# A fifth token tile routed by VectorE rows, and 18 places for expert weight pieces, in an attention, MLP and mixture-of-experts kernel

## The chip, the cores and the metric

One core of one Trainium2 chip. The metric is the device time of one execution in microseconds, of which the median over several runs is quoted. All arithmetic that matters is done at about fp32 accuracy: a large operand is split into a high part and a low part (names ending in `h` and `l`, or slices 0 and 1), and a product is three matmuls, high by high, high by low and low by high.

Engines: TensorE (PE: matmuls and transposes), VectorE (DVE), ScalarE (ACT), GpSimd (POOL) and SyncE (SP, which here issues the weight DMAs). Each of them runs its own instructions in the order in which they were built, and waits at an instruction whose inputs or buffers are not ready.

## The reference

Causal attention for 2 batches of 12 heads, 448 positions of 64; its output is x, 896 tokens of 768. Then a dense MLP, then a layer of eight experts, top one:

```python
h = np.maximum(x @ w_in, 0.0)              # 896 x 2048
x = h * h @ w_out                          # 896 x 768
xn = x / (np.linalg.norm(x, axis=-1, keepdims=True) + 1e-06)
en = expert_emb / (np.linalg.norm(expert_emb, axis=-1, keepdims=True) + 1e-06)
logits = xn @ en.T / tau                   # 896 x 8
expert_idx = np.argmax(logits, axis=1)
# gate_w: the softmax probability of the chosen expert
for e in range(E):
    mask = expert_idx == e
    h = np.maximum(x[mask] @ w1[e], 0.0)   # 768 -> 1024
    out[mask] = gate_w[mask, None] * (h @ w2[e])
```

## The kernel before

**Stages.** Attention and the first MLP matmul fill the first half of the time. The second MLP matmul (`b_tiles`) goes over seven tiles of 128 tokens: tiles 0 and 1 together, then tiles t = 2 to 6 one pass each. A pass has 16 steps f; a step is three pairs of matmuls, each 128x384 (`yps`, L639). After a pass ACT copies the sums to `ysb` (L648). After the passes come the experts, slot by slot (`hps`, `ops`).

**Routing.** A tile is routed by a generator, `route_tile` and then `choose`, whose PE instructions are put between the steps of the passes: tile t-1's logits are made in pass t, and its ranks follow in that pass or the next. A tile listed in `CFG["dve"]` gets its eight logits on DVE: eight instructions, each the product of the tile with one embedding row that is spread over all partitions (`rows`, L662). Any other tile gets them on PE: six transposes (`yt`, L672), a split of `yt` into `yhl` (ACT cast, DVE low part), six matmuls (`lgt`, L696), a DVE copy (`lgs`, L699) and two transposes (`lg`, L703). `choose` then takes the tile's norm by Newton steps (`norm_of`, L575 to L590, ten short DVE instructions after the start values), scales (`sc`, L712 to L715), finds the maximum `m`, lets ACT take the exponentials (`ex`, L720), and makes the one-hot rows `OH` (L725). PE counts ranks from `OH` (`rk`, L728), DVE reads them (`c8`, L740, and `ranks`).

**The early expert.** After the first five tiles (NE = 5) the expert with the most tokens among them is taken (`early`): PE counts (`cnt`, L794), DVE finds the expert's number `eidx` (L805) and which of its tokens go where (`oc`, L817; `rv`, L760), PE makes a table (`tabp`, L773), POOL gathers the tokens, and SP loads the expert's weights, whose number it reads from `eidx`. All that lies in passes 5 and 6, so that this expert's first matmuls (`hps`, slot "D") can follow the last pass at once.

**Weight pieces.** An expert's weights come in 16 pieces, two per DMA of 768 KB (`pieces`). ACT rounds a piece to its high part (`mh`), DVE makes the low part (`ml`). Each piece has a place, the buffers that a `w_out` piece held before, so there are 16. `pace` and `freed` limit how many pieces of later experts are fed ahead of the matmuls that read them.

**What sets the order.** PE's order is written out by hand: `CFG["rs"][t]` lists pairs (f, u), "at step f of pass t take the next part of tile u's routing"; `et` does that for `early` (steps of pass 5), `xe` for the gathered tokens and `ew` for weight pieces (steps of pass 6). The order on DVE, ACT, POOL and SP in these passes is made when the kernel is built, by a scheduler with its own model of durations; `urgent` raises the priority of routing, and `issue_after(last["oh"])` keeps the logits of a tile behind the `OH` of the tile before. The chunks `hs` are the MLP's hidden values of one tile and a quarter of the 16 steps, split by ACT and DVE (`h2_split`, L65 and L72) into one of four rotating buffers: the split for the next use of a buffer waits for the step that last reads it.

Of the kernel before, what the change touches and what calls it, by code (L numbers as in the profile page):

```python
# [8 lines left out]
F32 = mybir.dt.float32  # L9
# [23 lines left out]
def f32(ap):  # L33
# [20 lines left out]
def build(tc, qkd, vd, w_in, w_out, emb, tau, wm, cst, out, dbg_y=None):  # L54
# [452 lines left out]
    def wo_load():  # L507
        f = len(wo)
        wo.append(w_load(w_out, f, slots[woslot[f]], f"wo{f}", "woh", "wol"))

    def h2_split(t, q):

        hs = hpool.tile([P, 2, 4, P], F32R, tag="hs", bufs=4, name="hs")
        p0 = t * P
        at = p0
        while at < p0 + P:
            g = at // GT
            end = min(p0 + P, (g + 1) * GT)
# [103 lines left out]
    def b_tiles(ts, hooks={}):  # L622
        ps = {t: [ps_y.tile([P, 512], F32, tag=f"y{c}", name="yps") for c in range(2)] for t in ts}
        for f in range(NF):
            for x in hooks.get(f, ()):
                next(x, None)
            for _ in range(CFG["ew"].count(f) if -1 in hooks else 0):

                with ExitStack() as es:
                    if f > CFG["rt6"][3]:  # L630
                        es.enter_context(tc.issue_after(last["oh"].ins))
                    for _ in range(2):
                        next(hooks[-1], None)
# [156 lines left out]
    def early():  # L790
# [61 lines left out]
    def pieces(s, res):  # L852

        for i2 in range(8):
# [39 lines left out]
    def pace(x, cap=2.7):  # L894
# [241 lines left out]
    for t in range(2, NTI):  # L1136
# [10 lines left out]
        if t == NTI - 1:  # L1147
# [302 lines left out]
```

## Time and profile before

| | us |
|---|---|
| median of 3 runs (542.78 to 543.02) | 542.87 |
| the profiled execution | 543.2 |
| its span | 541.5 |
| PE busy | 527.2 (97%) |
| DVE busy | 413.5 (76%) |
| ACT busy | 287.4 (53%) |
| POOL busy | 205.6 (38%) |

The span is what the profile's times count from and to; the profiled execution is 1.7 us longer than its span and 0.3 us longer than the median. Starts below are microseconds from the start of the span. Pass 3 begins at 274.4, pass 4 at 291.5, pass 5 at 308.3, pass 6 at 328.2, and the early expert's matmuls at 348.3; PE's last matmul is at 532.8.

### The profile page before, as it was taken

What the parts mean: (1) busy time and instruction counts of PE and PEld (TensorE: products, weight loads), DVE (VectorE), ACT (ScalarE), POOL (GpSimd) and SP (SyncE); (2) the same over time, 40 slices, a digit from 0 to 9 for tenths busy, and PEclk for the clock granted to TensorE, in tenths of its full rate; (3) what the DMA queues carried; (4) which work ended last, traced back from release to release, by engine and by line L of the source; (5) the groups of instructions that cost most, each with busy time, mean ns of one, the idle gap of its engine ahead of it and who ended that gap; (6) DMA issues with size and microseconds to landing.
All of it is one profiled execution on the core that took longest, in us unless ns stands there. A gap on an engine that the chain in (4) does not pass through costs nothing.

```text
span 541.5 us, 9616 instructions
## 1 busy us (share of the span) xinstructions
PE 527.2 (97%) x3374; PEld 496.2 (92%) x3374; DVE 413.5 (76%) x976; ACT 287.4 (53%) x635; POOL 205.6 (38%) x273
## 2 busy tenths in 40 slices
PE   7899999999999999999999999999999999999993
PEld 4799999889999999999999989999999999999992
DVE  7888899656887979597899776895296897983741
ACT  7889887315335242433332326631386887764651
POOL 7998899916635643231011201026201302400010
PEclk9999999999999999999999999999999999999998
DMA  5667674331546555358200019303978889984310
GB/s 183 177 156 170 146 230 111 117 117 58 176 131 217 167 183 176 120 174 274 79 30 30 16 31 408 159 2 110 346 231 274 266 281 364 272 279 154 119 53 7
DMA packets 28474, 89.22 MB, mean 165 GB/s; under 512 B 2926, under 2 KB 12270, under 8 KB 28416
## 3 DMA queue, kind: packets, MB, share of 16 engines
q1 hardware_dynamic: 26880, 82.23, 47.8%
q0 software_dynamic: 1536, 6.29, 3.1%
q8 instruction: 28, 0.46, 0.3%
q14 instruction: 30, 0.25, 0.1%
HBM read 78.39 MB, written 6.32 MB: 156 GB/s over the span
## 4 chain that ended last, share of the span: by engine, by line
PE 73%; DVE 14%; DMA 6%; issue 2%; ACT 2%; POOL 2%; SPq 0%; POOLq 0%; DVEq 0%; ACTq 0%
PE yps L639 16%; PE ops L1048 11%; PE pv L323 7%; PE s L261 5%; PE pt L305 4%; DVE w L128 4%; DVE w L130 3%; PE hps L942 3%; PE ops L974 3%; PE ops L979 3%; DMA raw<-in_w_in 2%; PE pa L347 2%; PE pa L348 2%; PE pa L349 2%; DVE w L126 2%
## 5 line engine op out<-in xcount | busy, mean ns | idle before, releaser
L72 DVE TENSOR_TENSOR ml<-xraw,mh 128x768 fp32r<-128x768 f32 x64 | 59.4, 954 | 9.8 <-ACT mh L65 9.3
L65 ACT ACTIVATE mh<-xraw 128x768 fp32r<-128x768 f32 x64 | 52.1, 843 | 7.2 <-PE ops L974 5.8
L1048 PE MATMUL ops<-mh,act 128*128 128x384 f32 x224 | 53.5, 341 | 0.0
L323 PE MATMUL pv<-pt,v 128*128 128x448 f32 (+7 forms) x288 | 47.1, 296 | 0.6 <-ACT pt L65 0.6
L287 POOL TENSOR_SCALAR p<-p,rs 128x192 f32<-128x192 f32 (+6 forms) x84 | 45.5, 564 | 2.6 <-DVE rs L283 2.3
L274 ACT ACTIVATE p<-s,mn 128x192 f32<-128x192 f32 (+6 forms) x84 | 39.8, 476 | 11.7 <-DVE mn L271 6.4
L261 PE MATMUL s<-kh,q 128*128 128x128 f32 (+6 forms) x168 | 44.0, 308 | 0.7 <-ACT p L274 0.7
L130 DVE SCALAR_TENSOR_TENSOR w<-raw,w 128x768 int32<-128x768 int32 x32 | 42.5, 1331 | 0.7
L323 PEld LDWEIGHTS pv<-pt,v 128*128 128x128 f32 (+1 forms) x288 | 38.5, 163 | 2.7 <-ACT pt L65 1.2
L1048 PEld LDWEIGHTS ops<-mh,act 128*128 128x128 f32 x224 | 39.2, 188 | 0.8
L1074 POOL DMA_INDIRECT out<-osb,fsi x10 | 10.1, 1015 | 77.7 <-ACT osb L1069 48.8
L72 DVE TENSOR_TENSOR ml<-mraw,mh 128x768 fp32r<-128x768 f32 x32 | 30.1, 956 | 11.3 <-ACT mh L65 10.9
L128 DVE SCALAR_TENSOR_TENSOR w<-raw,w 128x768 int32<-128x768 int32 x32 | 37.0, 1160 | 0.7
L736 POOL CAST gh<-g 128x1 fp32r<-128x1 f32 x7 | 3.5, 505 | 88.1 <-DVE OHs L730 32.3
L126 DVE TENSOR_SCALAR w<-raw 128x768 int32<-128x768 int32 x32 | 22.9, 715 | 17.4 <-POOL wi3l L72 7.3
L72 DVE TENSOR_TENSOR pt<-pt 128x512 fp32r<-128x512 f32 x48 | 32.4, 683 | 4.8 <-ACT pt L65 4.8
L353 ACT ACTIVATE relu<-pa 128x448 f32<-128x448 f32 x32 | 17.0, 539 | 34.7 <-PE pa L349 34.7
L271 DVE CUSTOM_DVE_ANT_0 s<-s,maskf 128x192 f32<-128x192 f32 (+6 forms) x77 | 32.0, 430 | 4.5 <-PE s L261 4.4
L65 ACT ACTIVATE hs<-h 128x512 fp32r<-128x512 f32 (+1 forms) x32 | 17.8, 573 | 29.6 <-PE yps L639 27.5
L261 PEld LDWEIGHTS s<-kh,q 128*128 128x128 f32 x168 | 30.6, 197 | 2.6 <-ACT p L274 1.5
L72 DVE TENSOR_TENSOR hs<-h,hs 128x512 fp32r<-128x512 f32 (+1 forms) x32 | 21.9, 689 | 12.4 <-ACT hs L65 12.1
L65 ACT ACTIVATE pt<-pt 128x512 fp32r<-128x512 f32 x48 | 28.2, 600 | 5.6 <-PE pt L305 5.6
(471 smaller groups left out, 1681.3 us busy)
## 6 DMA issues: line engine op xcount, KB each, us to landing
xraw<-in_wm SPq DMA_DIRECT2D x32, 768.0 KB, 6.0
raw<-in_w_in SPq DMA_DIRECT2D x16, 768.0 KB, 4.2
raw<-in_w_out SPq DMA_DIRECT2D x16, 768.0 KB, 4.2
mraw<-in_wm SPq DMA_DIRECT2D x16, 768.0 KB, 4.7
qk<-in_qkd SPq DMA_DIRECT2D x11, 448.0 KB, 4.7
q<-qs SPq DMA_DIRECT2D x20, 224.0 KB, 3.8
v<-in_vd SPq DMA_DIRECT2D x12, 256.0 KB, 3.3
eb<-edram SPq DMA_DIRECT2D x8, 384.0 KB, 6.0
```

What stands on the lines that cost most here:

```text
L65: return A.activation(out, in_, AF.Copy, scale=scale)
L72: return eng.tensor_tensor(out=lo, in0=x, in1=hi, op=ALU.subtract)
L126: V.tensor_scalar(out=w[:, x], in0=raw[:, x, 1], scalar1=3, scalar2=0x3FFFFFFF, op0=ALU.logical_shift_left, op1=ALU.bitwise_and)
L128: V.scalar_tensor_tensor(out=w[:, x], in0=raw[:, x, 1], scalar=-0x40000000, in1=w[:, x], op0=ALU.bitwise_and, op1=ALU.bitwise_or)
L130: V.scalar_tensor_tensor(out=w[:, x], in0=raw[:, x, 0], scalar=29, in1=w[:, x], op0=ALU.logical_shift_right, op1=ALU.bitwise_or)
L261: T.matmul(ss, d["q2"][:, c, :, :, x].rearrange("p a b -> p (a b)"), d[y][:, :n], start=i_ == 0, stop=i_ == 2 and not first)
L271: last["max"] = V.tensor_tensor_reduce(out=ss, in0=ss, in1=maskf[:, S - n:], scale=-1.0, scalar=3.0e38, op0=ALU.add, op1=ALU.min, accum_ou ...
L274: last["exp", units.index(u), c] = A.activation(d["p"][c][:, :n], ss, AF.Exp, bias=mn, scale=1.0 if first else -1.0, accum_out=d["sm"][:, ...
L287: last["norm"] = G.tensor_scalar(out=p, in0=p, scalar1=rs[:, COL[c]:COL[c] + 1], scalar2=1.0, op0=ALU.mult, op1=ALU.mult)
L323: T.matmul(d["pv"][:, j * P:S] if h else d["pv"][0:D, j * P:S], d[x][:, j, 1:3].rearrange("p a b -> p (a b)") if h else d[x][:, j, 0], pt[ ...
L639: T.matmul(ps[t][c][:, :384], x, w[:, c * 384:(c + 1) * 384], start=(f == 0 and w is wh and x is hi), stop=(f == NF - 1 and x is lo))
L1048: T.matmul(ps[c], x, ww[:, col[c]], start=(fc == 0 and x is hh and ww is wh), stop=(fc == 7 and x is hl))
```

## The change

- Tile 4, the fifth, joins `CFG["dve"]`: its logits are eight DVE instructions and no longer PE's transposes and matmuls. Its embedding rows and the loads of them stay as they are, but rows 0 to 3 lie in four tiles of one row each instead of two tiles of two.
- The table `rs` for pass 5 has three entries where it had six: tile 4's parts now come at steps 1 and 12. `et` puts `early` at step 12 twice. So `rk` of tile 4 and `cnt` stand together at step 12, and `tabp` comes after step 15. `xe` moves four of its five entries one step later in pass 6. `ew` loses its last entry, and two weight pieces are issued ahead of pass 6.
- For every DVE tile `norm_of` is written ahead of the logits, inside the block that is held back to the `OH` of the tile before; it used to be written behind the logits and was free to start before.
- In pass 5 the `hs` splits of steps 7 and 11 are written at step 15, with that step's own; the low parts of these three are held behind `oc`, and that of step 3 behind tile 4's `OH`.
- 18 places for weight pieces: the first two are the embedding rows 0 to 3, the others the 16 old ones; `pace` may feed two pieces further.

```diff
-    first=1, hp=3000, xe=[1, 7, 8, 10, 12], turn=5, xfd=[3, 4, 5, 6], xfj=[1, 2, 3, 4],
-    joint=1, mhi="A", rt6=[1, 4, 7, 9, 15], dve=(0, 1, 2, 3), neng=(),
+    first=1, hp=3000, xe=[1, 8, 9, 11, 13], turn=5, xfd=[3, 4, 5, 6], xfj=[1, 2, 3, 4],
+    joint=1, mhi="A", rt6=[1, 4, 7, 9, 15], dve=(0, 1, 2, 3, 4), neng=(),
     rs={2: [(1, 0), (2, 1)], 3: [(2, 2), (2, 0), (10, 1)], 4: [(1, 3), (5, 2)],
-        5: [(2, 3), (2, 4), (3, 4), (4, 4), (5, 4), (7, 4)], 6: [(f, 5) for f in (1, 4, 7, 9, 15)]},
+        5: [(1, 4), (2, 3), (12, 4)], 6: [(f, 5) for f in (1, 4, 7, 9, 15)]},
     rd={2: [], 3: [0, 1], 4: [2], 5: [3, 4], 6: [5]},
-woh="A", h2h="A", h2l="V", et=[8, 8, 12],
-    ... ew=[2, 4, 10, 10, 10, 12], ...
+woh="A", h2h="A", h2l="V", et=[12, 12],
+    ... ew=[2, 4, 10, 10, 10], ...
@@ h2_split
-            lo_of(ENG[CFG["h2l"]], hs[:, 1, :, d], src, f32(hs[:, 0, :, d]))
+            with tc.issue_after(held[0].ins) if held else nullcontext():
+                lo_of(ENG[CFG["h2l"]], hs[:, 1, :, d], src, f32(hs[:, 0, :, d]))
@@ b_tiles
             if f % 4 == 3:
                 for t in ts:
-                    more_h2()
+                    if t == NE:
+                        held.append(last["oh" if f < 15 else "oc"])
+                    for _ in range({7: 0, 11: 0, 15: 3}.get(f, 1) if t == NE else 1):
+                        more_h2()
+                    held.clear()
@@ route_tile
             with tc.issue_after(last["oh"].ins) if t else nullcontext():
+                nrm = norm_of(rpool, ss, P, "yn", G if t in CFG["neng"] else None)
                 for x in range(E):
...
-            yield from choose(t, ss, l)
+            yield from choose(t, ss, l, nrm)
@@ pieces
-                pool, sl = slots[woslot[k]]
...
+                at = state["piece"] % (NF + 2)
+                state["piece"] += 1
+                if at < 2:
+                    pool, tags = epool, (f"e{2 * at}", f"e{2 * at + 1}")
+                else:
+                    pool, sl = slots[woslot[at - 2]]
+                    tags = f"s{sl}h", f"s{sl}l"
@@ pace
-        while fd["credit"] >= 1 and fd["done"] < min(fd["free"], 16 * (len(fd["seq"]) - 1)):
+        while fd["credit"] >= 1 and fd["done"] < min(fd["free"] + 2, 16 * (len(fd["seq"]) - 1)):
@@ the passes
             hooks[-1] = ewl
+            for _ in range(2):
+                next(ewl)
```

Three places of the built order, line numbers being those of each version.

**Place 1: DVE in pass 3, where tile 1 is routed.** `hs` is the low part of a split, `ynt` and `ynr` are Newton steps, `l`, `m`, `c` belong to `choose`. Before:

```order
L715 TENSOR_SCALAR l<-l,sc 128x8
L588 TENSOR_SCALAR ynt<-ynt 128x1
L717 TENSOR_REDUCE m<-l 128x1
L589 TENSOR_TENSOR ynr<-ynr,ynt 128x1
L718 TENSOR_SCALAR m<-m 128x1
L723 SCALAR_TENSOR_TENSOR c_3211<-l,m,ct 128x8
L587 SCALAR_TENSOR_TENSOR ynt<-ynr,ss 128x1
L72 TENSOR_TENSOR hs<-h_1_1786,hs 128x512
L724 TENSOR_REDUCE m<-c_3211 128x1
L588 TENSOR_SCALAR ynt<-ynt 128x1
L733 TENSOR_SCALAR g<-m 128x1
L725 TENSOR_SCALAR OH<-ct,m 128x8
```

and after the change:

```order
L593 TENSOR_TENSOR ynt<-ynr,ss 128x1
L72 TENSOR_TENSOR hs<-h_1_1786,hs 128x512
L724 TENSOR_SCALAR sc<-ynt 128x1
L725 RECIPROCAL sc<-sc 128x1
L726 TENSOR_TENSOR sc<-sc,rtau 128x1
L727 TENSOR_SCALAR l<-l,sc 128x8
L729 TENSOR_REDUCE m<-l 128x1
L730 TENSOR_SCALAR m<-m 128x1
L735 SCALAR_TENSOR_TENSOR c_3213<-l,m,ct 128x8
L736 TENSOR_REDUCE m<-c_3213 128x1
L745 TENSOR_SCALAR g<-m 128x1
L737 TENSOR_SCALAR OH<-ct,m 128x8
```

Before, `hs` stands behind most of `choose`, three instructions ahead of `OH`'s; now all of `choose` stands behind it. In pass 4 the same happens to tile 2: the low part of step 3's split, which stood behind tile 2's `OH`, among tile 3's logits, now stands ahead of it, behind the first two instructions of `choose`.

**Place 2: ACT in pass 5.** `ex_3787` (before) and `ex_3738` (after) are tile 4's exponentials, the rows L65 the high parts of `hs` splits. Before:

```order
L686 CAST yhl_3725<-yt_3714 128x3x128
L686 CAST yhl_3737<-yt_3718 128x3x128
L65 ACTIVATE hs_3746<-h2_1_1786 128x512
L720 ACTIVATE ex_3787,m_3784<-l_3763,m_3784 128x8
L65 ACTIVATE hs_3824<-h2_1_1786 128x512
L65 ACTIVATE hs_3879<-h2_1_1786 128x512
L648 COPY ysb_3929<-yps_3685 128x384
```

and after the change:

```order
L667 ACTIVATE sq_3697,ss_3696<-ysb_3684 128x768
L65 ACTIVATE hs_3775<-h2_1_1786 128x512
L65 ACTIVATE hs_3891<-h2_1_1786 128x512
L65 ACTIVATE hs_3894<-h2_1_1786 128x512
L732 ACTIVATE ex_3738,m_3735<-l_3699,m_3735 128x8
L658 COPY ysb_3900<-yps_3687 128x384
L65 ACTIVATE hs_3897<-h2_1_1786 128x512
```

`ex` stood behind one split of the pass and now stands behind three; the third (`hs_3894`) writes the buffer that steps 8 to 11 read.

**Place 3: PE and DVE around tile 4's ranks in pass 5.** PE, before:

```order
L639 MATMUL yps<-wo6h,hs 128x384 x2
L728 LDWEIGHTS tri
L728 MATMUL rk<-OH,tri 128x8
L729 LDWEIGHTS ones
L729 MATMUL rk<-OHs,ones 128x8
L639 MATMUL yps<-wo7h,hs 128x384 x2
L639 MATMUL yps<-wo7l,hs 128x384 x2
L639 MATMUL yps<-wo7h,hs 128x384 x2
L794 LDWEIGHTS ones
L794 MATMUL cnt_3827<-OHs,ones 128x8
```

and after the change:

```order
L645 MATMUL yps<-wo11h,hs 128x384 x2
L740 LDWEIGHTS tri
L740 MATMUL rk<-OH,tri 128x8
L741 LDWEIGHTS ones
L741 MATMUL rk<-OHs,ones 128x8
L806 LDWEIGHTS ones
L806 MATMUL cnt_3839<-OHs,ones 128x8
L645 MATMUL yps<-wo12h,hs 128x384 x2
```

DVE after the change, from tile 4's `OH` on:

```order
L745 TENSOR_SCALAR g<-m 128x1
L737 TENSOR_SCALAR OH<-ct,m 128x8
L72 TENSOR_TENSOR hs<-h_1_1786,hs 128x512
L746 RECIPROCAL g<-g 128x1
L742 TENSOR_TENSOR OHs<-OHs,OH 128x8
L752 TENSOR_TENSOR c_3740<-rk,OH 128x8
L753 TENSOR_REDUCE ranks<-c_3740 128x1
L808 COPY n_3841<-cnt_3839 128x8
```

`rk` moved from behind step 6 to behind step 11, and `cnt`, which had a step between, directly behind it. On DVE the instruction `g`, which reads what `ex` sums up, stands ahead of `OH` as before; an `hs` now stands between `OH` and the `c8` (here `c_3740`) that reads `rk`. Further down, two `hs` low parts now stand between `oc` and `rv`, where none stood before.

## Rows read from the trace of the kernel before

**Rows 1.** Busy us and instructions of each engine in windows, then clock, DMA share, GB/s.

```profile
18.00:20.00 2.00, 1.22 (x12) 1.11 (x12) 1.93 (x11) 1.83 (x8) 1.92 (x3) 1.00 0.33 66
...
324.00:326.00 2.00, 2.00 (x13) 2.00 (x14) 1.20 (x6) 0.33 (x1) 0.57 (x1) 1.00 0.80 301
...
538.00:540.00 2.00, 0.00 (x0) 0.00 (x0) 0.00 (x0) 0.00 (x0) 0.00 (x0) 0.50 0.03 8
```

**Rows 2.** The chain that ended last, pass 5: start, us, piece.

```profile
310.60 0.71 PE yt L672 x6
311.31 1.05 PE yps L639 x6
312.36 0.35 PE lgt L696 x3
...
313.79 0.02 issue
...
315.84 2.33 PE yps L639 x12
```

**Rows 3.** Timeline, PE: start, us, engine, line, operation, out<-in.

```profile
285.08 0.18 PE L728 MATMUL rk<-OH,tri 128*128 128x8 bf16 x1
...
296.69 0.18 PE L728 MATMUL rk<-OH,tri 128*128 128x8 bf16 x1
...
318.01 0.18 PE L728 MATMUL rk<-OH,tri 128*128 128x8 bf16 x1
...
323.50 0.61 PE L773 MATMUL tabp<-rv,ol 128*128 128x6 f32 x5
...
333.19 0.51 PE L696 MATMUL lgt<-yhl,ent 128*16 128x256 f32 x3
...
348.45 0.28 PE L961 MATMUL hps<-act,mh 128*128 128x256 f32 x1
```

**Rows 4.** Timeline, DVE; the bracket is idle time before and what ended it.

```profile
283.83 0.69 DVE L72 TENSOR_TENSOR hs<-h,hs 128x512 fp32r<-128x512 f32 x1 [0.96 <-ACT hs L65]
...
284.77 0.95 DVE L662 CUSTOM_DVE_ANT_0 sv<-ysb,eb 128x768 bf16<-128x768 f32 x1
...
292.94 0.08 DVE L662 DVE_READ_ACCUMULATOR2_ANT l<- 128x1 f32 x1
...
305.81 0.15 DVE L712 TENSOR_SCALAR sc<-ynt 128x1 f32<-128x1 f32 x1
...
306.86 0.15 DVE L718 TENSOR_SCALAR m<-m 128x1 f32<-128x1 f32 x1
...
317.59 0.22 DVE L725 TENSOR_SCALAR OH<-ct,m 128x8 bf16<-128x8 f32 x1
...
319.80 0.16 DVE L796 COPY n<-cnt 128x8 f32<-128x8 f32 x1
...
321.46 0.15 DVE L805 TENSOR_SCALAR eidx<-mx 128x1 int32<-128x1 f32 x1
...
330.41 0.96 DVE L72 TENSOR_TENSOR ml<-xraw,mh 128x768 fp32r<-128x768 f32 x1 [0.42 <-ACT mh L65]
...
347.01 0.55 DVE L72 TENSOR_TENSOR act<-xt,act 128x384 fp32r<-128x384 f32 x1
```

**Rows 5.** Timeline, ACT.

```profile
295.84 0.63 ACT L65 ACTIVATE hs<-h 128x512 fp32r<-128x512 f32 x1 [1.98 <-PE yps L639]
...
317.02 0.30 ACT L720 ACTIVATE ex<-l,m 128x8 f32<-128x8 f32 x1 [2.57 <-DVE m L718]
...
323.69 0.63 ACT L65 ACTIVATE hs<-h 128x512 fp32r<-128x512 f32 x1 [3.66 <-PE yps L639]
```

**Rows 6.** Timeline, SP: the early expert's first weight DMAs.

```profile
322.71 2.16 SPq L863 DMA_DIRECT2D xraw<-in_wm  x4
```

**Rows 7.** The page, part 6: DMA issues, KB each, median us to landing.

```profile
xraw<-in_wm SPq DMA_DIRECT2D x32, 768.0 KB, 6.0
...
raw<-in_w_out SPq DMA_DIRECT2D x16, 768.0 KB, 4.2
```

More of the change, by code (lines that the diff above doesn't have):

```diff
@@ L37 @@
 CFG = dict(
-    first=1, hp=3000, xe=[1, 7, 8, 10, 12], turn=5, xfd=[3, 4, 5, 6], xfj=[1, 2, 3, 4],
-    joint=1, mhi="A", rt6=[1, 4, 7, 9, 15], dve=(0, 1, 2, 3), neng=(),
+    first=1, hp=3000, xe=[1, 8, 9, 11, 13], turn=5, xfd=[3, 4, 5, 6], xfj=[1, 2, 3, 4],
+    joint=1, mhi="A", rt6=[1, 4, 7, 9, 15], dve=(0, 1, 2, 3, 4), neng=(),
     rs={2: [(1, 0), (2, 1)], 3: [(2, 2), (2, 0), (10, 1)], 4: [(1, 3), (5, 2)],
-        5: [(2, 3), (2, 4), (3, 4), (4, 4), (5, 4), (7, 4)], 6: [(f, 5) for f in (1, 4, 7, 9, 15)]},
+        5: [(1, 4), (2, 3), (12, 4)], 6: [(f, 5) for f in (1, 4, 7, 9, 15)]},
     rd={2: [], 3: [0, 1], 4: [2], 5: [3, 4], 6: [5]},
-woh="A", h2h="A", h2l="V", et=[8, 8, 12],
-    turn2=[1, 3], ft0=[(0, 3), (1, 2), (2, 0), (3, 3), (4, 1)], ft1=[3], ft2=[3, 5, 6, 7], late=[(2, 1), (4, 2)], ew=[2, 4, 10, 10, 10, 12], stop=0, xh="A", h2="A",
+woh="A", h2h="A", h2l="V", et=[12, 12],
+    turn2=[1, 3], ft0=[(0, 3), (1, 2), (2, 0), (3, 3), (4, 1)], ft1=[3], ft2=[3, 5, 6, 7], late=[(2, 1), (4, 2)], ew=[2, 4, 10, 10, 10], stop=0, xh="A", h2="A",
     wh="G", wil="G", wol="GV", warm=8, nsa=6, nwi=3, nwb=3, wo0=4, hs0=[4, 5, 8, 9], conv0=17, convs=2, pin=1,
@@ L509, in wo_load @@
         wo.append(w_load(w_out, f, slots[woslot[f]], f"wo{f}", "woh", "wol"))
+    held = []
     def h2_split(t, q):
@@ L603, in build @@
     for x in range(0, E, 2):
-        r = (epool if x < E // 2 else spool).tile([P, 2, DM], F32, tag=f"e{x}" if x < E // 2 else "raw", name="eb")
+        if x < E // 2:
+            rows += [epool.tile([P, DM], F32, tag=f"e{x + j}", name="eb") for j in range(2)]
+        else:
+            r = spool.tile([P, 2, DM], F32, tag="raw", name="eb")
+            rows += [r[:, j] for j in range(2)]
         for j in range(2):
-            DMA.dma_start(out=r[:, j], in_=edram[x + j:x + j + 1, :].broadcast_to([P, DM]))
-            rows.append(r[:, j])
+            DMA.dma_start(out=rows[x + j], in_=edram[x + j:x + j + 1, :].broadcast_to([P, DM]))
     enp = ps_r.tile([P, KC, E], F32, tag="lg", name="enp")
@@ L706, in route_tile, with choose @@
         yield from choose(t, ss, l)
-    def choose(t, ss, l):
-        nrm = norm_of(rpool, ss, P, "yn", G if t in CFG["neng"] else None)
+    def choose(t, ss, l, nrm=None):
+        if nrm is None:
+            nrm = norm_of(rpool, ss, P, "yn", G if t in CFG["neng"] else None)
         sc = rpool.tile([P, 1], F32, tag="sc", bufs=2, name="sc")
@@ L816, in early @@
         V.tensor_tensor(out=oc[:, :, 1], in0=ise, in1=half, op=ALU.mult)
-        V.tensor_tensor(out=oc[:, :, 0], in0=ise, in1=oc[:, :, 1], op=ALU.subtract)
+        last["oc"] = V.tensor_tensor(out=oc[:, :, 0], in0=ise, in1=oc[:, :, 1], op=ALU.subtract)
         yield from table(oc, NE, 3, 2, lane, "e")
@@ L837, in h_at @@
         return hb[..., 0:n], hb[..., n:2 * n]
-    state = dict(raw=0, bank=0, routed=False)
+    state = dict(raw=0, piece=0, bank=0, routed=False)
     def bank(name):
@@ L865, in pieces @@
                 k = 2 * i2 + j
-                pool, sl = slots[woslot[k]]
-                hi = pool.tile([P, DM], F32R, tag=f"s{sl}h", name="mh")
-                lo = pool.tile([P, DM], F32R, tag=f"s{sl}l", name="ml")
+                at = state["piece"] % (NF + 2)
+                state["piece"] += 1
+                if at < 2:
+                    pool, tags = epool, (f"e{2 * at}", f"e{2 * at + 1}")
+                else:
+                    pool, sl = slots[woslot[at - 2]]
+                    tags = f"s{sl}h", f"s{sl}l"
+                hi, lo = (pool.tile([P, DM], F32R, tag=x, name=n) for x, n in zip(tags, ("mh", "ml")))
                 x = raw[:, j * DM:(j + 1) * DM]
```

## The prediction

> **What bounds the kernel now.** I read the busy times by window first. From pass 3 to the last matmul TensorE is busy in practically all of every window, as in the middle row of [rows 1], while no other engine is. So in this half only two things change the time: what PE no longer executes, and how long PE comes to stand at an instruction whose input is late. The chain of waits says the same: in pass 5 it runs through PE almost without a break, and leaves it at one place, between a step of tile 4's logits and the next [rows 2]. Then I took, for each matmul that reads a routing result, the start on PE's timeline [rows 3] and followed its producers on DVE and ACT [rows 4, 5] in the changed order, each engine strictly in its own order and each operation with its traced duration. All starts are of the profiled execution (543.2 us); the median is 0.33 lower, and I take that off at the end.
>
> **What is removed.** Tile 4's PE work in pass 5, from the chain [rows 2]: the six transposes 0.71, the first three `lgt` 0.35. From 313.79, the end of the third step's matmuls, to 315.84 there are 2.05 us, in which stand one step of `yps` (six matmuls, 1.05 by the row at 311.31) and the rest: the second `lgt`, two waits of PE for ACT and DVE, and `lg`; that is 1.00. Together 2.06, so **-2.1 us**. The ACT casts and DVE low parts of `yhl` go too, at no gain on PE. In their place DVE has eight logits; nobody waits for them but `OH`. How long they take: tile 2's eight run from 284.77 to 292.94 + 0.08, 8.25 us for eight [rows 4].
>
> **What is added.** PE executes nothing new; all that is added is waits. To price them I need three lengths. From `sc` to the maximum `m` (L718) DVE takes 306.86 - 305.81 = 1.05 [rows 4], six short dependent instructions, 0.2 each; so a Newton chain of seven, the part that remains behind the logits, takes about 1.4 (an estimate). From `ex` on ACT to the end of `OH` on DVE, where `g` stands ahead of `OH`, it is 317.59 + 0.22 - 317.02 = 0.79 [rows 4, 5]; with 0.2 from `m` to `ex` that makes `sc` to `OH`'s end 2.0. A DVE low part `hs` is 0.69 long [rows 4]; rows of one engine overlap by some 0.08 at their ends, so I count 0.6 (an estimate).
>
> *Tile 1, pass 3.* DVE's `hs` at 283.83 waited 0.96 for ACT [rows 4]. Before, the whole of `choose` but its last four rows had run in front of it. Now all of it stands behind (place 1): 283.83 + 0.6 + 2.0 = 286.45, and `rk` was at 285.08 [rows 3]. PE waits **1.4**. If ACT has `ex` done sooner the `g` ahead of `OH` costs nothing and it is 1.1.
>
> *Tile 2, pass 4.* Tile 2's logits, pinned behind `OH` of tile 1, start 1.6 later than 284.77, at 286.4, and end at 294.65. An `hs` (0.6), seven Newton steps (1.4) and two rows of `choose` (0.4) bring DVE to about 297.1. There an `hs` waits for its high part, which ACT makes when PE's fourth step ends: 295.84 [rows 5] plus the 1.4 that PE is late by now, plus 0.63, is 297.9. Behind it 0.6 and the rest of `choose`, 1.6: `OH` is done at 300.2. PE would be at `rk` at 296.69 + 1.4 = 298.1 [rows 3]. It waits **2.1**. Even without that `hs`, 297.1 + 1.6 = 298.7 leaves 0.6.
>
> *Tile 3, pass 5.* Its `OH` was long done in pass 4; now an `hs` that waits for ACT's copies of the sums stands ahead. By the same reckoning **0.1**, at most 0.4.
>
> *Tile 4, pass 5.* Call T the time when PE ends step 11 (323.50 before [rows 3]). ACT has `ex` behind a split that writes the buffer which steps 8 to 11 read (place 2), so it waits for that: the split runs from T + 0.19 (323.69 - 323.50, [rows 3, 5]) to T + 0.82, `ex` starts at T + 0.75, `OH` is done 0.79 later, and `rk` starts at about T + 1.57. Behind `OH` DVE has `hs` (0.6), two short rows and the `c8` that reads `rk`; `cnt` writes the same PSUM buffer (one buffer for all tiles tagged `lg`), so it waits for that read: T + 2.4. `cnt` was hidden behind a step before; now PE waits **2.3** in all. The lower bound has another cause: tile 4's logits start behind `OH` of tile 3, and with Newton and `sc` to `m` they reach `ex` at about T + 0.5, so at least 1.5 remains even if ACT were free.
>
> *Table, pass 5.* DVE copies `cnt` at about T + 2.6, and `eidx` came 321.46 - 319.80 = 1.66 after that copy [rows 4], with an `hs` in it where now the table's `ol` and two other rows stand: T + 4.6 with 0.3 for these. Another 0.9 goes to `oc` (five short instructions); then two `hs` (1.2) stand ahead of `rv`: T + 7.1. PE, with four steps of 1.05 behind `cnt`, is at `tabp` at T + 6.7. **0.4**, between 0 and 0.8.
>
> *The early expert's loads.* The first weight DMA needs `eidx`, and came 322.71 - 321.46 = 1.25 later [rows 4, 6], 0.8 ahead of T. Now it comes at T + 4.6 + 1.25 = T + 5.85, so 6.6 later as PE counts; PE itself is later by 2.3 + 0.4 = 2.7 behind T. The loads fall back by 3.9 against PE. Two places feel it. First `lgt` in pass 6, because ACT has two `mh` ahead of tile 5's first cast and DVE two `ml` (0.96 each) ahead of its low part. With landing after 4.4 (DMAs of this size have medians of 4.2 and 6.0 [rows 7]), that is at T + 10.25, one `mh` (0.85, an estimate from `ml` of the same shape, less the overlap) and two `ml` end at T + 12.9, and `yhl`'s low part (0.55, as the row of the same shape at 347.01) at T + 13.4. PE is there at 333.19 - 323.50 = 9.7 after T [rows 3], plus 2.3 + 0.4 and 0.1 for `rk` and `cnt` themselves: T + 12.5. **0.9**. With 4.2 it is 0.7, with 6.0 it is 2.5, but whatever falls here is missing from the next place. There, at the second `hps` (348.45 [rows 3]), the low part of the gathered tokens (347.01 + 0.55 [rows 4], 0.9 ahead of PE) stands behind six `ml` whose pieces land 3.9 - 0.9 = 3.0 later as PE counts: 3.0 less the 0.7 to 0.9 of slack, **2.2** (1.0 to 3.0).
>
> **The 18 places and the pace.** They could let pieces of later experts be made earlier. PE has no wait for a piece in that part, so this is worth **0**. A loss is bounded by the DVE and ACT work that it pulls forward, which is the same work: 0 to 0.3.
>
> **The sum.** -2.1 + 1.4 + 2.1 + 0.1 + 2.3 + 0.4 + 0.9 + 2.2 = +7.3. 543.2 + 7.3 = 550.5, less 0.33: **550.2 us**. The lower ends (1.1, 0.6, 0, 1.5, 0, and 2.0 for both loads) make +3.1, 546.0; they don't fall together. The upper ends (1.6, 2.4, 0.4, 2.6, 0.8, and 4.0) make +9.7, 552.6. The order of instructions is certain, the durations are traced; what is least certain is whether waits shift each other, because a later term shrinks when an earlier one grows.
>
> **Rivals.** *A: PE gets past the waiting `rk`.* If a matmul that waits for `OH` did not hold the `yps` behind it, all five waits would vanish from PE's time and only the removal would count: 542.87 - 2.1 = 540.8. The point from which it decides: a `yps` of the next step that starts before `rk`. Against it: at 313.79 PE had `yps` of the next step at hand, with its operands there, and still stood for `lgs` until `lg` had run [rows 2]. Chance 0.04. This is the case that ends on the other side.
>
> *B: only the routing waits arise and the loads catch up.* If the pieces and the gathered tokens land some 3 us sooner against their issue than I take it, the last two terms go: 550.2 - 3.1 = 547.1. For it: only the gathers compete with them. Against it: a DMA of this size has not shown a median under 4.2 [rows 7], and the first six are issued close together as before. Chance 0.10.
>
> *C: TensorE's clock falls.* PE had no waits of 1.4 to 2.3 us in these passes. The granted clock stayed at 1.00 even where PE was busy only 1.22 of 2.00 us, and fell to 0.50, the lower of its two levels (1.2 GHz), only after the last matmul [rows 1]. If it fell after the wait at tile 4 and stayed low for the four steps that are left of pass 5, they would take 4.2 more: 554.4. Chance 0.05. The Trainium skill, TensorE: Matmul & The Clock Gate, in the section on HAM oscillation, states that a kernel in which PE idles between bursts of matmuls loses its full clock; by it this change, which puts five pauses where there were two short ones, goes the way of C, while the trace so far bears out that short pauses are harmless.
>
> *D: the change does less than it says.* If the DVE chain is in time at tiles 1 and 2 (because ACT's split comes earlier than in the trace), 3.5 of the sum goes: 546.7. For it only that these two waits hang on one ACT row each; against it, that this row hangs on PE's own step. Chance 0.05.
>
> **How the numbers follow.** The forecast (waits at all five places, 548 to 552) has 0.74, A 0.04, B 0.10, C 0.05, D 0.05, and 0.02 for no change from causes not seen. The range takes in the forecast's own, B and part of D: 546.9 to 552.2. A measurement of this kernel can tell about 0.2%, 1.1 us, from no change. Faster by more than that is A and a little of the unseen: 0.05; within it 0.03; slower 0.92.
>
> **What would show it.** In the profile of the changed kernel: no `yt` and `lgt` in pass 5; PE idle before `rk` of tile 1 (1.4), of tile 2 (2.1) and of tile 4 (1.6, and 0.8 more at `cnt`), released by DVE's `OH` and `c8`; 0.4 before `tabp`; idle of some tenths before the first `lgt` of pass 6, and some two microseconds between the first two `hps`; the rest of the profile shifted by 7.3 and otherwise as before, the clock at 1.00. It is wrong if `rk` of tiles 1 and 2 starts without idle time, or if the first `hps` follows the last `yps` as closely as before, with its second at once behind it.

## The result, and the profile after

The changed kernel takes 550.56 us (median of 4 runs, 549.53 to 551.15) against 542.94; the ratio is 1.0133, with a 95% interval of 1.0121 to 1.0146 (the two medians alone give 1.0140). The profiled execution took 551.15 (543.2 before) with a span of 549.4 (541.5). PE is busy as long as before (527.4 us against 527.2); the time went into PE standing still. One execution each of the kernels e3 and e8 below took 2926 and 1811 us, several times the others, and is left out of their medians and ratios; e8's profile is of that execution, so its waits are read from e10, the same kernel again.

The list of PE's waits in the profile after (what waited for what: us in total, times, the longest), over the whole span, the lines of passes 3 to 6 and the first expert; the list of before has none there:

```profile
PE rk L740 <- DVE ynr L578: 3.1, 2, 1.9
PE hps L978 <- DVE act L72: 2.1, 1, 2.1
...
PE rk L740 <- DVE OH L737: 1.4, 1, 1.4
...
PE lgt L707 <- DVE yhl L72: 0.8, 1, 0.8
...
PE cnt L806 <- DVE c L752: 0.6, 1, 0.6
```

The releaser in the first line, `ynr`, is a start value of the next tile's norm that stands directly behind `OH` and ends some 0.05 after it; the input that `rk` needs is `OH`. DVE's rows ahead of the two waits, tile 1 and tile 2:

```profile
283.76 0.69 DVE L72 TENSOR_TENSOR hs<-h,hs 128x512 fp32r<-128x512 f32 x1 [1.07 <-ACT hs L65]
...
286.10 0.22 DVE L737 TENSOR_SCALAR OH<-ct,m 128x8 bf16<-128x8 f32 x1
286.23 0.14 DVE L578 TENSOR_SCALAR ynr<-ss 128x1 int32<-128x1 int32 x1
...
297.77 0.69 DVE L72 TENSOR_TENSOR hs<-h,hs 128x512 fp32r<-128x512 f32 x1 [0.83 <-ACT hs L65]
...
299.78 0.22 DVE L737 TENSOR_SCALAR OH<-ct,m 128x8 bf16<-128x8 f32 x1
```

The same waits on PE's timeline after, in the order of [rows 3] (`rk` of tiles 1, 2, 3 and 4, then `cnt`, `tabp`, `lgt` and the first two `hps`):

```profile
286.37 0.17 PE L740 MATMUL rk<-OH,tri 128*128 128x8 bf16 x1 [1.19 <-DVE ynr L578]
...
300.06 0.17 PE L740 MATMUL rk<-OH,tri 128*128 128x8 bf16 x1 [1.95 <-DVE ynr L578]
...
314.00 0.17 PE L740 MATMUL rk<-OH,tri 128*128 128x8 bf16 x1
...
326.24 0.17 PE L740 MATMUL rk<-OH,tri 128*128 128x8 bf16 x1 [1.40 <-DVE OH L737]
...
327.04 0.17 PE L806 MATMUL cnt<-OHs,ones 128*128 128x8 bf16 x1 [0.61 <-DVE c L752]
...
331.44 0.72 PE L785 MATMUL tabp<-rv,ol 128*128 128x6 f32 x5
...
337.94 0.52 PE L707 MATMUL lgt<-yhl,ent 128*16 128x256 f32 x3 [0.85 <-DVE yhl L72]
...
353.01 0.28 PE L977 MATMUL hps<-act,mh 128*128 128x256 f32 x1
...
355.40 0.39 PE L978 MATMUL hps<-act,mh 128*128 128x256 f32 x1 [2.11 <-DVE act L72]
```

Read against [rows 3], each start gives how late PE is by then. `rk` of tile 1 is 286.37 - 285.08 = 1.29 late, that of tile 2 3.37, that of tile 3 3.60 (without a wait), the first `lgt` of pass 6 4.75, the second `hps` 355.40 - 348.45 = 6.95. The bracket counts from the modelled end of the matmul before, so it is 0.1 to 0.2 less than the step in these differences.

The last line of [rows 1] had the lower clock only after the last matmul. In the profile after, the windows around tile 2's `rk` and around the second `hps` (busy us and instructions of PE, PEld, DVE, ACT and POOL; then clock, DMA share, GB/s) are these:

```profile
298.00:300.00 2.00, 0.11 (x1) 0.04 (x1) 1.66 (x11) 0.40 (x2) 0.00 (x0) 1.00 0.00 0
354.00:356.00 2.00, 0.60 (x5) 0.60 (x6) 1.97 (x7) 0.86 (x2) 0.00 (x0) 1.00 0.50 197
356.00:358.00 2.00, 2.00 (x13) 2.00 (x12) 0.59 (x5) 0.48 (x1) 0.00 (x0) 0.58 0.00 0
358.00:360.00 2.00, 2.00 (x13) 2.00 (x12) 1.84 (x8) 1.95 (x4) 0.00 (x0) 0.57 0.01 4
360.00:362.00 2.00, 2.00 (x20) 1.87 (x19) 0.72 (x4) 1.75 (x4) 0.00 (x0) 1.00 0.02 4
```

After the pause before the second `hps` the granted clock is near the lower of its two levels for some 3.5 us, and in the two windows of 0.58 and 0.57 PE gets 13 matmuls done where the next one has 20. That cost is on top of 6.95. The 18th matmul of the early expert, the last one at the low clock, shows how much it is (first after, then before):

```profile
359.52 0.37 PE L979 MATMUL hps<-act,ml 128*128 128x256 f32 x1
```

```profile
351.21 0.28 PE L962 MATMUL hps<-act,ml 128*128 128x256 f32 x1
```

It is 8.31 late, so the clock cost 1.4. The span is only 549.4 - 541.5 = 7.9 longer: some 0.4 is regained in what follows.

### The profile page after: what moved, and what is told of

Its sections match the earlier page's. It is cut to its first block, busy times and chain, and to the rows that moved or that the text cites. A ratio compares the mean times of both kernels' runs of the same rounds, so it can differ in the third digit from the quotient of the medians.

```text
span 549.4 us, 9589 instructions
## 1 busy us (share of the span) xinstructions
PE 527.4 (96%) x3359; PEld 497.4 (91%) x3360; DVE 421.7 (77%) x988; ACT 286.3 (52%) x633; POOL 208.7 (38%) x273
## 2 busy tenths in 40 slices
DMA packets 28472, 89.21 MB, mean 162 GB/s; under 512 B 2926, under 2 KB 12270, under 8 KB 28416
## 4 chain that ended last, share of the span: by engine, by line
PE 76%; DVE 11%; DMA 6%; ACT 2%; POOL 2%; issue 2%; SPq 0%; POOLq 0%; DVEq 0%; ACTq 0%
PE yps L645 12%; PE ops L1065 11%; PE pv L323 6%; PE pa L347 6%; PE pa L348 6%; PE pa L349 6%; PE s L261 4%; PE pt L305 3%; PE hps L959 3%; DMA mraw<-in_wm 3%; PE ops L996 3%; PE ops L991 3%; DVE w L128 2%; PE hps L977 2%; PE hps L978 2%; PE hps L979 2%
## 5 line engine op out<-in xcount | busy, mean ns | idle before, releaser
L65 ACT ACTIVATE mh<-xraw 128x768 fp32r<-128x768 f32 x64 | 51.5, 840 | 6.0 <-PE ops L991 4.0
L287 POOL TENSOR_SCALAR p<-p,rs 128x192 f32<-128x192 f32 (+6 forms) x84 | 44.0, 542 | 3.1 <-DVE rs L283 2.9
L673 DVE CUSTOM_DVE_ANT_0 sv<-ysb,eb 128x768 bf16<-128x768 f32 x40 | 36.9, 951 | 0.0
L65 ACT ACTIVATE hs<-h 128x512 fp32r<-128x512 f32 (+1 forms) x32 | 17.8, 574 | 35.5 <-PE yps L645 35.5
L126 DVE TENSOR_SCALAR w<-raw 128x768 int32<-128x768 int32 x32 | 24.1, 753 | 15.3 <-POOL wi3l L72 7.2
L65 ACT ACTIVATE pt<-pt 128x512 fp32r<-128x512 f32 x48 | 28.2, 599 | 5.6 <-PE pt L305 5.6
```

What stands on the lines that cost most here:

```text
L65: return A.activation(out, in_, AF.Copy, scale=scale)
L287: last["norm"] = G.tensor_scalar(out=p, in0=p, scalar1=rs[:, COL[c]:COL[c] + 1], scalar2=1.0, op0=ALU.mult, op1=ALU.mult)
```

## The experiments

The kernel before ran beside each group of kernels on the same chip, each group on another one: 543.38 beside e1 to e4, 543.91 beside e5 to e8, 543.20 beside e9 to e11. Ratios are against these. A pause or wait of PE is given as its list has it.

**e1: `norm_of` behind the logits again.** The theory was that the Newton steps and the `hs` which now stand ahead of `OH` make the waits of tiles 1 and 2; the rivals, that tile 4's logits do, or that waits only move.

```
-                nrm = norm_of(rpool, ss, P, "yn", G if t in CFG["neng"] else None)
...
-            yield from choose(t, ss, l, nrm)
+            yield from choose(t, ss, l)
```

> The changed kernel with one thing undone: norm_of is written behind the logits again (in choose), as before the change. Theory (PE waits for OH, and the Newton steps and the hs that now stand ahead of OH are why): the waits at rk of tile 1 (1.36) and tile 2 (2.11) go, 3.5 us together; the waits at rk and cnt of tile 4, at lgt and at the second hps stay, since they hang on T, PE's own step 11, and shift with it: 550.6 - 3.5 = 547.1, or 546 if the granted clock, which fell to 0.58 behind the second hps, stays at 1.00. Rival (tile 4's eight logits on DVE push the whole chain back, wherever the Newton steps stand): the two waits stay and the time is within 0.5 of 550.6. Second rival (the waits only move): rk of tile 4 then waits 3.5 less and all later waits grow, 550.

Measured: 547.74, ratio 1.0076 (1.0055 to 1.0098), single runs between 545.43 and 550.13. All PE's waits from 256 us on in its profile:

```profile
PE hps L977 <- DVE act L72: 2.1, 1, 2.1
PE rk L739 <- DVE OH L736: 1.4, 1, 1.4
PE lgt L706 <- DVE yhl L72: 0.8, 1, 0.8
PE cnt L805 <- DVE c L751: 0.6, 1, 0.6
PE tabp L784 <- DVE rv L771: 0.2, 1, 0.2
```

The two waits are gone and the others stand as they were, to a tenth: so the place of `norm_of` makes these 3.1 us of waits (3.4 of lateness), and the rest is independent of it. By the ratios the time fell by 3.1 (1.33% less 0.76% of 543), which the intervals don't tell from the 3.5 expected. In this profile too the clock fell behind the second `hps` (0.79, 0.50 and 0.86 in the windows from 352 to 358).

**e2: the kernel before, with `norm_of` ahead of the logits and nothing else.** The edit is that of e1 in the other direction, put into the kernel before.

> The kernel before with one part of the change alone: norm_of is written ahead of the logits inside the block held behind the OH of the tile before, for tiles 0 to 3; tile 4 stays on PE, 16 places. Theory: PE waits 1.4 at rk of tile 1 and 2.1 at rk of tile 2, nothing else changes (tile 4's route runs on PE with its own slack, and the loads shift with PE): 542.9 + 3.5 = 546.4. Rival (the fifth tile's DVE logits are needed for the waits): within 0.5 of 542.9. If the later part absorbs the shift, as where DVE or DMAs were ahead of PE by more, 543 to 545.

Measured: 546.31, ratio 1.0057 (1.0039 to 1.0075). One line is left in the list of PE's waits from 256 us on, `rk` for 3.1 in two pieces. This part alone makes the waits of tiles 1 and 2, without a fifth tile on DVE.

**e3: the kernel before, with the 18 places, the longer pace and the changed `ew` alone, two pieces issued ahead of pass 6.**

> The kernel before with the other part alone: 18 places for pieces (two in embedding rows 0 to 3), the pace allowed two pieces further, two pieces issued ahead of pass 6 and the last entry of ew dropped; tile 4 on PE and norm_of as before. Theory: PE has no wait for a piece in the experts, so 542.9 within 0.5. Rival (the places bring the gain that the change was worth, hidden in the changed kernel under its waits): faster by 1 or more. Other rival (early expert's pieces ahead of tile 5's cast cost at lgt or hps): slower by 0.5 to 1.5.

Measured: 543.59 against 543.38, ratio 1.0005 (0.9992 to 1.0017). PE has two short new waits (0.4 before a `yt`, 0.3 before `tabp`). No gain or loss by the places can be told in this kernel, where PE has no wait for a piece.

**e4: `rk` of tiles 1 and 2 three and four steps later.** The question was whether only PE's order was wrong.

```
-    ... 3: [(2, 2), (2, 0), (10, 1)], 4: [(1, 3), (5, 2)],
+    ... 3: [(2, 2), (2, 0), (13, 1)], 4: [(1, 3), (9, 2)],
```

> The changed kernel with PE's rank matmuls of tile 1 three steps later (13 instead of 10 of pass 3) and of tile 2 four steps later (9 instead of 5 of pass 4); norm_of and all else as in the change. Theory A (the DVE chain tile after tile is itself too long, since each tile's logits are held behind the OH before): no wait at these two, but DVE is late anyhow and PE waits 2 to 3.2 at rk of tile 3, which was 0.1: gain of 0.3 to 1.5, to 549.1 to 550.3. Theory B (only the place of the rk was wrong): the 3.5 us go without a new wait, 547.1.

Measured: 547.92, ratio 1.0097 (1.0063 to 1.0130). PE's two longest waits from 256 us on:

```profile
PE rk L740 <- DVE ynr L578: 3.0, 1, 3.0
PE hps L978 <- DVE act L72: 1.8, 1, 1.8
```

The first is now tile 3's `rk`. The 3.1 us that PE no longer waits at tiles 1 and 2 come back as 3.0 at the next tile. That is theory A's mechanism, and DVE's times show it: `OH` of tiles 1, 2 and 3 starts at 286.06, 299.45 and 313.23 here and at 286.10, 299.78 and 313.71 in the change, though PE's `rk` stand elsewhere; before they were at 284.63, 295.38 and 307.37. Each tile's logits are held behind the `OH` before, so with the Newton steps behind the logits each tile adds to the lateness. The time is 1.2 below theory A's range. The waits of the whole list sum to 6.8 against 8.0 in the change, as tile 4's `rk` waits 0.4 instead of 1.4; and in this profile the clock stayed at 1.00 behind a pause of 1.85 before the second `hps`, where it cost 1.4 in the change.

**e5: the pause before the second `hps` filled.** 18 transposes of the identity on PE, ahead of the first `hps`.

```
+    dm = ps_y.tile([P, 512], F32, tag="y0", name="dm")
+    for i in range(18):
+        T.transpose(dm[:, (i % 4) * P:(i % 4 + 1) * P], ident, ident)
```

> The changed kernel with 18 extra transposes of the identity on PE (128x128 fp32, 0.11 us each by the gather's transposes xt, 2.0 us together, results unused) between pass 6 and the first hps, where PE otherwise stands 2.1 us behind the first hps. Theory (the granted clock fell to 0.58 over some 4 us because PE stood still there, and that cost 1.2 us): the first hps starts 2 us later and the second at once behind it, at the same time as before the fill; the clock stays at 1.00 after it; 550.6 - 1.2 = 549.4, runs closer together. Rival (the clock falls for another reason, the longer waits of pass 3 to 5 added up): the clock still falls near 356 and the time stays at 550.6. Second rival (the extra transposes cost their own 2 us): 552.5.

Measured: 550.62, ratio 1.0127 (1.0083 to 1.0172), runs from 549.27 to 553.77. Inconclusive as to the time, but its windows tell something that was not asked:

```profile
326.00:328.00 2.00, 0.41 (x4) 0.34 (x4) 1.28 (x8) 0.53 (x3) 0.28 (x2) 0.93 0.00 0
328.00:330.00 2.00, 2.00 (x7) 2.00 (x8) 1.97 (x12) 0.00 (x0) 0.23 (x2) 0.50 0.00 0
330.00:332.00 2.00, 2.00 (x10) 2.00 (x9) 1.90 (x8) 0.00 (x0) 0.00 (x0) 0.72 0.16 25
...
356.00:358.00 2.00, 1.25 (x11) 1.06 (x10) 1.97 (x6) 0.20 (x2) 0.00 (x0) 1.00 0.50 197
358.00:360.00 2.00, 2.00 (x20) 2.00 (x18) 1.72 (x11) 1.09 (x3) 0.00 (x0) 1.00 0.00 0
```

With the pause cut to 0.74 the clock stays up behind the second `hps`. But now it fell behind `rk` and `cnt` of tile 4, at waits of 1.40 and 0.61 that are the same as in the changed kernel, where it had stayed up. From `cnt` to `tabp` PE took 5.8 instead of 4.4 us, so this fall cost 1.4. The wait of 0.8 before `lgt` is gone in turn.

**e6: the early expert's weights taken from expert 0.** The DMAs no longer wait for `eidx`.

> The changed kernel, but the early expert's weights are those of expert 0, whatever the routing says, so that SP's DMAs don't wait for eidx (its tokens are still the routed ones; this leaves out the choice of the weights). Theory (lgt and the second hps wait because pieces land late, so ml stands late ahead of the low parts): the waits before lgt (0.85) and the second hps (2.11) go, the clock stays at 1.00, the waits at the three rk and at cnt stay: 550.6 - 3.0 - 1.2 = 546.4, or up to 1 more if earlier pieces put mh and ml ahead of tile 4's routing. Rival (the gathered tokens or PE's transposes are what is late at hps): that wait stays, 549.5 to 550.6.

Measured: 548.50, ratio 1.0096 (1.0073 to 1.0120). All PE's waits from 256 us on:

```profile
PE rk L740 <- DVE ynr L578: 3.1, 2, 1.9
PE rk L740 <- DVE OH L737: 2.1, 1, 2.1
PE cnt L806 <- DVE c L752: 0.6, 1, 0.6
```

Both waits that were put down to late pieces are gone (0.85 and 2.11), and the clock stays at 1.00; so it is the pieces, not the gathered tokens, and through `eidx` the routing of tile 4. Of the 4.2 expected 2.0 show by the ratios and 3.2 between the two profiled spans. For a part of the shortfall the cause is on the timelines: pieces that land early bring `mh` and `ml` into pass 5, two `ml` among tile 4's logits, and its `rk` waits 0.7 longer.

**e7: as e1, with `rk` of tile 4 at step 14 and `cnt` and `tabp` later.**

```
-        5: [(1, 4), (2, 3), (12, 4)], ...
+        5: [(1, 4), (2, 3), (14, 4)], ...
...
-    ... et=[12, 12],
+    ... et=[14, 15],
```

> As e1 (the changed kernel with norm_of behind the logits), and rk of tile 4 at step 14 instead of 12 of pass 5, cnt at 14, tabp one part later. Theory (the waits at rk and cnt are PE standing in a chain that runs from tile 4's sums through logits, OH, count, table and loads; moving PE's matmuls later moves the wait, since all that follows starts later): no wait at rk, but 2 to 4 us before tabp and 2 to 4 before the lgt pair, 548.5 to 550 in all, that is 1 to 3 more than e1. Rival (PE simply comes too early at step 12): the waits of 1.4 and 0.6 go, 545 to 546.

Measured: 547.61, ratio 1.0070 (1.0051 to 1.0088), e1's within the intervals. All PE's waits from 256 us on:

```profile
PE tabp L784 <- DVE ynr L578: 3.6, 1, 3.6
PE lgt L706 <- DVE yhl L72: 0.7, 1, 0.7
```

No wait at `rk`, at `cnt` or at the second `hps`; one of 3.6 at `tabp`, and the clock at 0.55 and 0.59 behind it. The sum of the waits, 4.3, compares with 5.1 in e1. The wait moved along the chain, as the theory had it, though without the second one before `lgt` that it also named, and e7 is not slower than e1.

**e8 and e10: as e1, `cnt` one step behind `rk`, the later gathered tiles one step later.** (`et=[13, 13]`, `xe=[1, 9, 10, 12, 14]`.)

> As e1, and cnt one step behind rk (et at 13, so a step of yps covers c8's read of rk, 0.6) and the four later xe entries one step later (9, 10, 12, 14; so the casts of the gathered tokens stand behind more pieces). Theory: rk waits 1.4 as in e1, cnt no longer; tabp about 1.2 more; the second hps under 1, so the clock stays at 1.00: 545 to 546, faster than e1's median by 2, still slower than before. Rival (only the sum of the chain counts): as e1, 547.5.

> The kernel of e8 once more, for an undisturbed profile: rk of tile 4 waits 1.4, cnt not at all, tabp 1.2 to 1.5, lgt 0.8, the second hps under 1.0 because the later transposes of the gathered tokens cover it; clock at 1.00 there. If the clock falls in this execution it is behind the rk or tabp wait, as in e5.

Measured: e8 545.35, ratio 1.0024 (1.0012 to 1.0035); e10, one execution of the same kernel, 545.33. PE's waits in e10 are 1.4 at `rk`, 1.3 at `tabp`, 0.7 at `lgt`, 0.4 at a transpose of the gathered tokens, and none at `cnt` or `hps`. Its clock is at 1.00 from 18 us to the last matmul (from 12 to 18 us, in attention, it was down to 0.50). By the ratios these entries of PE's order are worth some 2.8 us against e1; the waits make 1.3 of that, 3.8 against 5.1, and a clock that no longer falls can be the rest. What `et` and what `xe` does was not separated.

**e9: every wait shortened by order alone.** On top of e1: the high parts of the held `hs` splits also held behind tile 4's `ex`; `rv` made with `oc`, the low parts held behind `rv`; `et=[13, 13]`, `xe=[1, 9, 11, 13, 15]`, tile 5's third part at step 8.

```
-            copy_on(ENG[CFG["h2h"]], hs[:, 0, :, d], src)
+            with tc.issue_after(last["ex"].ins) if held else nullcontext():
+                copy_on(ENG[CFG["h2h"]], hs[:, 0, :, d], src)
...
-                        held.append(last["oh" if f < 15 else "oc"])
+                        held.append(last["oh" if f < 15 else "rv"])
```

> Built on the changed kernel, every wait that was found shortened by order alone: norm_of behind the logits; in pass 5 the high parts of the held hs splits (ACT) also held behind tile 4's ex; rv written together with oc, and the three low parts held behind rv instead of oc; cnt one step behind rk (et 13); tile 5's third part at step 8 instead of 7 of pass 6; gathered tokens' transposes at 1, 9, 11, 13, 15. Theory (each wait is an instruction that stands ahead of its reader in a queue, and only what the chain of tile 4's logits takes is left): rk of tile 4 waits about 0.7 (DVE's own chain, as reckoned in the prediction: T + 0.5), cnt 0, tabp under 0.5, lgt under 0.5, the second hps under 0.3, clock at 1.00; against the removal of 2.1 that leaves 0.3 to 1.0 faster than before. Rival (tile 4's logits on DVE cost at least what they save, by the length of the chain): the waits turn up elsewhere, before the gathered tokens' transposes or the first expert's matmuls, 0.5 to 2 slower than before.

Measured: 543.03 against 543.20, ratio 0.9992 (0.9983 to 1.0001): no difference that can be told. All PE's waits from 256 us on:

```profile
PE xt L1116 <- DVE act L72: 1.0, 1, 1.0
PE rk L740 <- DVE OH L737: 0.4, 1, 0.4
PE tabp L788 <- DVE rv L773: 0.4, 1, 0.4
PE lg L714 <- DVE lgs L710: 0.3, 1, 0.3
```

The waits at `rk`, `cnt`, `lgt` and `hps` shrank or went as the theory said. But one of 1.0 appeared where the rival put it, at the last transpose of the gathered tokens: the waits sum to 2.1, about as much as was removed. By the ratios this kernel is 7.7 us faster than the change (1.33% and 0.08% of 543), and no faster than the kernel before.

**e11: the change without its pins.** The `hs` splits at steps 7, 11 and 15 again, nothing held.

> The changed kernel without its pins in pass 5: the hs splits written at steps 7, 11 and 15 again and their low parts held behind nothing. Theory (rk of tile 4 hangs on ACT's and DVE's hs rows that stand ahead of ex and OH; the pins keep DVE's low parts out of the way): without them these rows stand ahead of OH and eidx, rk waits 2 to 3.4 instead of 1.4, and the loads come later: 0.5 to 2 slower than the changed kernel. Rival (the pins are what puts three splits ahead of ex and so make the wait): rk waits 0.5 or less, 1 faster than the changed kernel.

One execution: 551.11, beside 551.15 for the profiled execution of the change. `rk` of tile 4 waits 3.2 instead of 1.4, within the theory's range, but `cnt` waits 0.3, `lgt` 0.2 and the second `hps` not at all, so the time hardly differs, where 0.5 to 2 more were expected. The pins do shorten the wait at `rk`. That the time is the same has to do with the clock, one window of which is this:

```profile
332.00:334.00 2.00, 2.00 (x8) 2.00 (x8) 0.22 (x2) 0.00 (x0) 0.00 (x0) 0.50 0.42 80
```

It fell behind `rk` and was at 0.50 from 328 to 334; from `cnt` (328.99) to `tabp` (335.81) PE took 6.8 instead of 4.4, so this fall cost 2.4. `eidx`, and so the loads, come 1.95 later than in the change, but PE reaches `tabp` 4.4 later; that fits the small waits behind it. At the second `hps` (356.77) e11 is 1.4 behind the change, and there the change's own fall of the clock costs it 1.4. One execution can't tell what the pins are worth in time.

## Why the prediction was right, and where it was not

The forecast was 550.2 and +7.3 against the profiled execution of before; measured are 550.56 and, between the two profiled executions, +7.95. Term by term, in PE's lateness as read above:

| term | predicted | measured |
|---|---|---|
| tile 4's PE work removed | -2.1 | -2.4 |
| `rk` of tile 1 | +1.4 | +1.3 |
| `rk` of tile 2 | +2.1 | +2.1 |
| `rk` of tile 3 | +0.1 | +0.2, no wait |
| `rk` of tile 4 and `cnt` | +2.3 | +2.3 |
| `tabp` | +0.4 | +0.2 |
| first `lgt`, pass 6 | +0.9 | +1.0 |
| second `hps` | +2.2 | +2.2 |
| TensorE's clock | 0 | +1.4 |
| all that follows | 0 | -0.4 |

For the first row: PE ends step 11 of pass 5 at 324.69 (the ACT split below starts 0.19 later, as in [rows 3, 5]), 1.19 late against 323.50, where it was 3.60 late at tile 3's `rk`. The waits alone, without the clock, came out 0.35 below the forecast's 7.3; the clock, which the sum had at nothing, brought the total to 7.9. So the mechanism of the waits was right, term by term, and that the total came so close is partly luck.

*The chain at tile 4.* It is there row by row. First ACT, then DVE, after:

```profile
324.88 0.63 ACT L65 ACTIVATE hs<-h 128x512 fp32r<-128x512 f32 x1 [3.60 <-PE yps L645]
325.41 0.29 ACT L732 ACTIVATE ex<-l,m 128x8 f32<-128x8 f32 x1
```

```profile
324.17 0.15 DVE L730 TENSOR_SCALAR m<-m 128x1 f32<-128x1 f32 x1
...
325.89 0.15 DVE L745 TENSOR_SCALAR g<-m 128x1 f32<-128x1 f32 x1 [1.24 <-ACT ex L732]
325.96 0.22 DVE L737 TENSOR_SCALAR OH<-ct,m 128x8 bf16<-128x8 f32 x1
326.09 0.68 DVE L72 TENSOR_TENSOR hs<-h,hs 128x512 fp32r<-128x512 f32 x1
...
326.83 0.16 DVE L752 TENSOR_TENSOR c<-rk,OH 128x8 f32<-128x8 f32 x1
...
328.91 0.14 DVE L817 TENSOR_SCALAR eidx<-mx 128x1 int32<-128x1 f32 x1
...
331.20 0.18 DVE L772 TENSOR_TENSOR rv<-oc,vals 128x30 fp32r<-128x30 f32 x1
```

With T = 324.69, `ex` starts at T + 0.72 (0.75 predicted), `rk` at 326.24 = T + 1.55 (1.57), `cnt` at 327.04 = T + 2.35 (2.4). `m`, which `ex` needs, is ready at 324.3, ahead of T, where the prediction had DVE's own chain reach `ex` at T + 0.5; so here ACT's split made this wait, and the lower bound of 1.5, for which the prediction gave DVE's own chain as the cause, was wrong. e9 bears that out: of e1 and e9, which both have `norm_of` behind the logits, e1 has the split ahead of `ex` and waits 1.4 at `rk`, e9 has it behind and waits 0.4.

*The table.* Here the size was wrong. `eidx` came at T + 4.2, not 4.6, because the allowance of 0.3 for the table's `ol` was not needed, `ol` having taken the place of an `hs`. The prediction's own terms, 4.6 + 0.9 + 1.2, make 6.7 and not the 7.1 that it states for `rv`; `rv` itself (0.18) was not among them. It ran from T + 6.5 to T + 6.7, just as PE ended step 15 (T + 6.6), and `tabp` starts at T + 6.75. The two `hs` ahead of `rv` are there, and cost next to nothing.

*The loads.* First weight DMA at 330.17, T + 5.5 (5.85 predicted); ACT has the first piece 4.3 later (4.4 predicted). The gathered tokens' low part stands behind six `ml`, as forecast; the last three of them and the row itself:

```profile
352.19 2.69 DVE L72 TENSOR_TENSOR ml<-mraw,mh 128x768 fp32r<-128x768 f32 x3
354.79 1.01 DVE L72 TENSOR_TENSOR act<-xt,act 128x384 fp32r<-128x384 f32 x2
```

That it is late pieces that hold the first `lgt` and the second `hps` is shown by e6.

*Tiles 1 and 2.* Shown by e1, where undoing one line removes both waits, and by e2, where that line alone makes them. The rows are where the prediction had them: `OH` is done at 286.32 and 300.00 (286.45 and 300.2 predicted).

*The clock.* Rival C had a chance of 0.05 and a place, behind tile 4's `rk`, and a price of 4.2. In the profiled execution of the change it happened, at the second `hps`, for 1.4; at tile 4 it happened in e5, for 1.4, and in e11, for 2.4. The chance was far too low and the price too high: the low clock lasted some 3.5 us in the change and under 6 in e11, and where it came early a part of its cost was taken off the waits behind it (e5, e11). So the forecast of a clock at 1.00 failed, in an execution at the upper end of the four runs. The Trainium skill (TensorE: Matmul & The Clock Gate, the section on HAM oscillation) tells of a kernel whose matmuls, after each wait for a DMA, start again at the lower clock. The runs agree that waits between matmuls can lose the clock (0.58 behind 2.11, 0.50 behind 1.40 and 0.61), though not in every execution; the waits in that example are longer than those of the change, so what it says of C is weaker than the prediction makes it, and that pauses of 2 us can do it is shown by these runs.

*The rest.* Rivals A, B and D did not happen: no `yps` passes a waiting `rk`, the loads did not catch up, and DVE was not in time. (What PE stood for at 313.79, in the argument against A, was `yhl`'s low part; it stood for `lgs` one step later.) For the places 0 was forecast, and e3 agrees.

## What to carry to other kernels

Before work is moved off the bound engine onto one with idle time, follow the moved chain to the next instruction of the bound engine that reads its result, in the queues' order: here 2.4 us were saved on PE, and about 9 us of lateness before its matmuls were made (8.0 as the list of waits has it), by an engine that is busy 77% of the time. A line that changes sides of a block of long instructions in one queue (seven short Newton steps that came to stand behind eight logits) can cost more than the work that a change saves, so look at what stands right ahead of the value that others wait for. And when PE's reader is moved later to cover a wait, look for the wait at the next reader: most of it turned up there in e4 and e7. Less was left where PE had a step of other work between two readers (e10), or where what feeds the chain started earlier (e9).

## What was not expected of the hardware

The granted clock is not the same from execution to execution behind the same pause. Behind waits of 1.40 and 0.61 at tile 4 it stayed at 1.00 in the change and fell to 0.50 in e5; behind 2.13 and 0.61 in e6 it stayed. Behind the second `hps` it fell after 2.11 (the change) and 2.06 (e1) and stayed after 1.85 (e4). Longer waits don't settle it either: it fell after 3.6 in e7 and 3.2 in e11, but stayed after 3.0 at tile 3 in e4. What decides it stays open. The falls that can be priced cost 1.4 (the change, e5) and 2.4 (e11).

Kernels with such pauses have wider runs: 545.43 to 550.13 for e1, against 542.25 to 543.92 for e9, whose longest wait from 256 us on is 1.0. That the clock makes the spread is shown only in part. In e4 the run of 551.08 has a mean granted clock of 0.989 and the other three, 547.62 to 547.98, have 0.995 or 0.996; but e1's fastest and slowest run both have 0.992.
